# Moving a preparation phase behind the first matmuls, and splitting one sine into two, in a fused FFT-filter and state-space kernel

## Chip, cores, metric

One Trainium2 chip, one core. The metric is device time in microseconds (us) from the first to the last instruction. The runs of one kernel agree within about 0.3%. A profile shows one of these runs, so its span differs a little from the median.

TensorE is written PE in the profile lines, its weight loads PEld, VectorE DVE, ScalarE ACT, GpSimd POOL. "Granted clock" is the share of TensorE's full clock that the throttle allowed, as the records show it.

## The reference, cut to what matters

The kernel computes an output and twelve gradients of a gated sum of two branches:

```python
g = sigmoid((x * gate_w).sum(-1))
a = irfft2(rfft2(x) * (w_r + 1j * w_i))          # branch A: 2-D FFT filter, S=2048, D=1024
P = exp((dt * A)[:, :, None] * arange(L))        # branch B: state space, N=128 states
K = einsum("dn,dnl,dn->dl", C, P, dt * B).real
b = fft_convolve(K, u) + u * Dskip
out = g * a + (1 - g) * b                        # and its vjp for 12 inputs
```

In the kernel the FFTs are matmuls with cosine and sine tables. Phase A is branch A, in two passes (forward and gradient). A pass has four stages; I call the first one the projection. Phase B is branch B: 8 blocks of 128 channels. In the middle of each block lies what I call the SSM stage, in which complex powers are made from an exponential and a sine/cosine pair, 8 channels (a sub-block) at a time. AtR and AtJ are the real and imaginary parts of these powers.

## The kernel before

The three places that the change touches. First, every table comes from one helper: three VectorE operations and one sine.

```python
def trig_gen(dst, c, F, u0, us, modN, cos, tmp_pool, eng=None):
    ...
    nc.vector.tensor_scalar(out=t_i[:], in0=viota[:, 0:F], ...)            # angle, integer
    nc.vector.tensor_single_scalar(out=k_i[:], in_=t_i[:], scalar=modN - 1, op=ALU.bitwise_and)
    nc.scalar.activation(out=dst, in_=k_i[:], func=ACT.Sin, scale=-TWO_PI / modN, bias=pi_b[:])
```

Second, the head of the program. It prepares phase B first, then a barrier, then the tables of phase A, then the projection.

```python
if CFG["phaseB"]:                                  # preparation for phase B
    with ExitStack() as qctx:
        ... # 16 tables of 1025 columns (PBq_c, PBq_s) -> DRAM scratch
        def load_Tq(tl, src, i_t):                 # called 6 times: 48 x (load, transpose, copy)
            for dc in range(DC):
                eng.dma_start(out=rb[:], in_=src[dc * P:(dc + 1) * P, :])
                nc.tensor.transpose(ptq[:, :], rb[:, :], ident[:, :])
                ... # copy out on VectorE or ScalarE
        ... # products of the parameters -> DRAM scratch
    tc.strict_bb_all_engine_barrier()
if CFG["phaseA"]:
    with ExitStack() as actx:
        psum = actx.enter_context(tc.tile_pool(name="psumA", bufs=2, space=bass.MemoryType.PSUM))
        ...
        for c in range(DC):
            trig_gen(PA_c[:, c, :], ...); trig_gen(PA_s[:, c, :], ...)
        for c in range(MC):
            trig_gen(OA_c[:, c, :], ...); trig_gen(OA_s[:, c, :], ...)     # not used by the projection
```

Third, the SSM stage. A block has 4 groups (`tg`) of 4 sub-blocks (`sbl`).

```python
for tg in range(NTG):
    Tsb = bm.tile([P, DG, 4, C16], dt.bfloat16, name="Tsb")
    EAg = bm.tile([P, TG, Ds * N], dt.bfloat16, name="EAg")                # pool: one buffer
    for sbl in range(TG):
        pz0, pz1 = bcast_rows(zr2_scr, dg0, "pE", "pF")
        nc.scalar.activation(out=EAg[:, sbl, 0:HNF], in_=pz0[:, :], func=ACT.Exp, ...)
        nc.scalar.activation(out=EAg[:, sbl, HNF:2 * HNF], in_=pz1[:, :], func=ACT.Exp, ...)
    for sbl in range(TG):
        pp0, pp1 = bcast_rows(phi2_scr, dg0, "pG", "pH")
        Ts = ssmp.tile([P, Ds * N], dt.int32, name="Ts")                   # one buffer
        ... # two ScalarE copies PSUM -> Ts
        FsFc = ssmp.tile([P, 2, Ds * N], dt.int32, name="FsFc")            # one buffer
        nc.vector.tensor_single_scalar(out=FsFc[:, 0, :], in_=Ts[:], ..., op=ALU.bitwise_and)
        nc.vector.tensor_single_scalar(out=Ts[:], in_=Ts[:], ..., op=ALU.add)
        nc.vector.tensor_single_scalar(out=FsFc[:, 1, :], in_=Ts[:], ..., op=ALU.bitwise_and)
        scv = ssmp.tile([P, 2, Ds * N], dt.bfloat16, name="scv")           # one buffer
        nc.scalar.activation(out=scv[:], in_=FsFc[:], func=ACT.Sin, ...)   # both halves at once
        nc.vector.tensor_tensor(out=AtR[:], in0=EAg[:, sbl, :], in1=scv[:, 1, :], op=ALU.mult)
        nc.vector.tensor_tensor(out=AtJ[:], in0=EAg[:, sbl, :], in1=scv[:, 0, :], op=ALU.mult)
        for q in range(Ds // NQ):
            ... # 4 x (transpose of AtR, transpose of AtJ), 2 copies to Ad, 24 small matmuls
        ... # KT_blk <- psK on VectorE; Tsb <- psT on ScalarE
    # end of the group: products and reductions over the four sub-blocks
    nc.vector.tensor_tensor(out=p1[:], in0=Bcat1[:, gdl, :, :], in1=T12, op=ALU.mult)
    nc.vector.tensor_reduce(out=res4[:, 0, :], in_=p1[:]..., axis=AX.X, op=ALU.add)
    ... # three more such pairs, and T3 = T12 * erow + T34
```

Of the kernel before, what the change touches and what calls it, by code (L numbers as in the profile page):

```python
# [10 lines left out]
dt = mybir.dt  # L11
ACT = mybir.ActivationFunctionType
ALU = mybir.AluOpType
# [6 lines left out]
def kernel(  # L20
# [10 lines left out]
    nc = tc.nc  # L31
    P = 128
# [89 lines left out]
    if CFG["phaseB"]:  # L122
        with ExitStack() as qctx:
            psQ = qctx.enter_context(tc.tile_pool(name="psumQ", bufs=1, space=bass.MemoryType.PSUM))
            qpool = qctx.enter_context(tc.tile_pool(name="q_const", bufs=1))
            PBq_c = qpool.tile([P, MC, SH + 1], dt.bfloat16, name="PBq_c")
            PBq_s = qpool.tile([P, MC, SH + 1], dt.bfloat16, name="PBq_s")
            with tc.tile_pool(name="trig_tmpQ", bufs=2) as ttmp:
                for c in range(MC):
                    trig_gen(PBq_c[:, c, :], c, SH + 1, 0, 1, S, True, ttmp)  # L130
                    trig_gen(PBq_s[:, c, :], c, SH + 1, 0, 1, S, False, ttmp)
            nc.sync.dma_start(out=pb_scr[0, :, :], in_=PBq_c[:].rearrange("p a b -> p (a b)"))
            nc.scalar.dma_start(out=pb_scr[1, :, :], in_=PBq_s[:].rearrange("p a b -> p (a b)"))

            def load_Tq(tl, src, i_t):
                with tc.tile_pool(name=f"ldTq{i_t}", bufs=2) as ldp:
                    for dc in range(DC):
                        rb = ldp.tile([P, N], dt.bfloat16, name="ldT_rows")
                        eng = nc.sync if (i_t + dc) % 2 == 0 else nc.scalar
                        eng.dma_start(out=rb[:], in_=src[dc * P:(dc + 1) * P, :])  # L140
                        ptq = psQ.tile([P, P], dt.bfloat16, name=("qG" if dc % 2 == 0 else "qH"))
                        nc.tensor.transpose(ptq[:, :], rb[:, :], ident[:, :])
                        if dc % 2 == 0:
                            nc.vector.tensor_copy(out=tl[:, dc * P:(dc + 1) * P], in_=ptq[:, :])
                        else:
                            nc.scalar.activation(out=tl[:, dc * P:(dc + 1) * P], in_=ptq[:, :], func=ACT.Copy)
            ArTq = qpool.tile([P, D], dt.bfloat16, name="ArTq")
            AiTq = qpool.tile([P, D], dt.bfloat16, name="AiTq")
            load_Tq(ArTq, B_A_re, 0)
            load_Tq(AiTq, B_A_im, 1)  # L150
            nc.sync.dma_start(out=nlb_scr[0, :, :], in_=ArTq[:])
            nc.scalar.dma_start(out=nlb_scr[1, :, :], in_=AiTq[:])
            zr_q = qpool.tile([P, D], dt.float32, name="zr_q")
            phi_q = qpool.tile([P, D], dt.float32, name="phi_q")
            wR_q = qpool.tile([P, D], dt.float32, name="wR_q")
            wJ_q = qpool.tile([P, D], dt.float32, name="wJ_q")
            with tc.tile_pool(name="wtmp", bufs=1) as wtmp:
                dt_b0 = wtmp.tile([P, D], dt.float32, name="dt_b0")
                nc.gpsimd.dma_start(out=dt_b0[:], in_=B_log_dt.partition_broadcast(P))
                nc.scalar.activation(out=dt_b0[:], in_=dt_b0[:], func=ACT.Exp)  # L160
                nc.vector.tensor_tensor(out=zr_q[:], in0=dt_b0[:], in1=ArTq[:], op=ALU.mult)
                nc.vector.tensor_tensor(out=phi_q[:], in0=dt_b0[:], in1=AiTq[:], op=ALU.mult)
                nc.vector.tensor_scalar(out=phi_q[:], in0=phi_q[:], scalar1=-1.0 / TWO_PI, scalar2=None, op0=ALU.mult)
                BrT0 = wtmp.tile([P, D], dt.bfloat16, name="BrT0")
                BiT0 = wtmp.tile([P, D], dt.bfloat16, name="BiT0")
                CrT0 = wtmp.tile([P, D], dt.bfloat16, name="CrT0")
                CiT0 = wtmp.tile([P, D], dt.bfloat16, name="CiT0")
# [4 lines left out]
                dBr = wtmp.tile([P, D], dt.float32, name="dBr")  # L172
                dBi = wtmp.tile([P, D], dt.float32, name="dBi")
                nc.vector.tensor_tensor(out=dBr[:], in0=dt_b0[:], in1=BrT0[:], op=ALU.mult)
                nc.vector.tensor_tensor(out=dBi[:], in0=dt_b0[:], in1=BiT0[:], op=ALU.mult)
                t1 = wtmp.tile([P, D], dt.float32, name="t1")
                t2 = wtmp.tile([P, D], dt.float32, name="t2")
                nc.vector.tensor_tensor(out=t1[:], in0=CrT0[:], in1=dBr[:], op=ALU.mult)
                nc.vector.tensor_tensor(out=t2[:], in0=CiT0[:], in1=dBi[:], op=ALU.mult)
                nc.vector.tensor_tensor(out=wR_q[:], in0=t1[:], in1=t2[:], op=ALU.subtract)  # L180
                nc.vector.tensor_tensor(out=t1[:], in0=CrT0[:], in1=dBi[:], op=ALU.mult)
                nc.vector.tensor_tensor(out=t2[:], in0=CiT0[:], in1=dBr[:], op=ALU.mult)
                nc.vector.tensor_tensor(out=wJ_q[:], in0=t1[:], in1=t2[:], op=ALU.add)
                nc.vector.tensor_scalar(out=wJ_q[:], in0=wJ_q[:], scalar1=-1.0, scalar2=None, op0=ALU.mult)
                nc.sync.dma_start(out=nl_scr[0, :, :], in_=zr_q[:])
                nc.scalar.dma_start(out=nl_scr[1, :, :], in_=phi_q[:])
                nc.sync.dma_start(out=nl_scr[2, :, :], in_=wR_q[:])
                nc.scalar.dma_start(out=nl_scr[3, :, :], in_=wJ_q[:])
                ldt = wtmp.tile([P, DC], dt.float32, name="ldt")
                nc.gpsimd.dma_start(out=ldt[:], in_=B_log_dt.rearrange("(c p) -> p c", p=P))  # L190
                nc.scalar.activation(out=ldt[:], in_=ldt[:], func=ACT.Exp)
                nldt = wtmp.tile([P, DC], dt.float32, name="nldt")
                nc.vector.tensor_scalar(out=nldt[:], in0=ldt[:], scalar1=-1.0 / TWO_PI, scalar2=None, op0=ALU.mult)
                with tc.tile_pool(name="dl_tmp", bufs=2) as dtmp:
                    for dc in range(DC):
                        ar = dtmp.tile([P, N], dt.bfloat16, name="ar")
                        ai = dtmp.tile([P, N], dt.bfloat16, name="ai")
                        nc.sync.dma_start(out=ar[:], in_=B_A_re[dc * P:(dc + 1) * P, :])
                        nc.scalar.dma_start(out=ai[:], in_=B_A_im[dc * P:(dc + 1) * P, :])
                        for (srcb, sclt, dstscr) in ((ar, ldt, zr2_scr), (ai, nldt, phi2_scr)):  # L200
                            vf = dtmp.tile([P, N], dt.float32, name="vf")
                            nc.vector.tensor_scalar(out=vf[:], in0=srcb[:], scalar1=sclt[:, dc:dc + 1], scalar2=None, op0=ALU.mult)
                            vhi = dtmp.tile([P, N], dt.bfloat16, name="vhi")
                            nc.vector.tensor_copy(out=vhi[:], in_=vf[:])
                            vlo = dtmp.tile([P, N], dt.bfloat16, name="vlo")
                            nc.vector.tensor_tensor(out=vlo[:], in0=vf[:], in1=vhi[:], op=ALU.subtract)
                            nc.sync.dma_start(out=dstscr[0, dc * P:(dc + 1) * P, :], in_=vhi[:])
                            nc.scalar.dma_start(out=dstscr[1, dc * P:(dc + 1) * P, :], in_=vlo[:])
        tc.strict_bb_all_engine_barrier()

    if CFG["phaseA"]:
        with ExitStack() as actx:
# [6 lines left out]
            with tc.tile_pool(name="trig_tmp", bufs=2) as ttmp:  # L219
# [3 lines left out]
                for c in range(MC):  # L223
                    trig_gen(OA_c[:, c, :], c, SH, 1, 2, S, True, ttmp)
                    trig_gen(OA_s[:, c, :], c, SH, 1, 2, S, False, ttmp)
# [14 lines left out]
            def run_pass(bwd: bool):  # L240
                with ExitStack() as pctx:
                    x1pool = tc.alloc_tile_pool(name="x1pool", bufs=1, side="right")
                    X1 = x1pool.tile([P, 2, MC, NCOL], dt.bfloat16, name="X1")
                    with tc.tile_pool(name="xtpool", bufs=1, side="right") as xtpool, tc.tile_pool(name="xcpool", bufs=3, side="right") as xcpool:
# [3 lines left out]
                        for pi in range(2):  # L248
                            for mc in range(MC):
# [8 lines left out]
                                for dg in range(0, DC, TB):  # L258
                                    nb = min(TB, DC - dg)
                                    ptq = psum.tile([P, TB, P], dt.bfloat16, name="pt_tr")  # L260
# [6 lines left out]
                        for pi in range(2):  # L267
                            for mc in range(MC):
# [8 lines left out]
                                for (kind, kb) in blocks:  # L277
                                    if kind == "N":
                                        pt = psum.tile([P, 2], dt.float32, name="pt_n")
# [22 lines left out]
                                if CFG.get("dbg"):  # L302
                                    dbg = CFG["dbg"]
                                    rr = (pi * MC + mc) * P
                                    nc.sync.dma_start(out=dbg[6 if bwd else 5][rr:rr + P, :], in_=X1[:, pi, mc, :])
                    zpool = tc.alloc_tile_pool(name="zpool", bufs=1, side="left")
                    Zt = zpool.tile([P, 2, 2, QC, NCOL], dt.bfloat16, name="Zt")
                    with tc.tile_pool(name="t2y", bufs=2, side="right") as ypool, tc.tile_pool(name="t2w", bufs=2, side="right") as wpool, \
                            tc.tile_pool(name="t2e", bufs=2, side="right") as epool:
                        for rho in range(2):  # L310
                            for qc in range(QC):
# [49 lines left out]
                                pN = psum.tile([P, 8], dt.float32, name="pt_n")  # L361
# [213 lines left out]
    if CFG["phaseB"]:  # L575
# [13 lines left out]
        with ExitStack() as bctx:  # L589
# [177 lines left out]
            for bi in range(NBLK):  # L767
# [82 lines left out]
                with tc.tile_pool(name="ssm", bufs=1, side="right") as ssmp, tc.tile_pool(name="ssm2", bufs=2, side="right") as ssm2, \  # L850
# [11 lines left out]
                    for tg in range(NTG):  # L862
                        Tsb = bm.tile([P, DG, 4, C16], dt.bfloat16, name="Tsb")
                        EAg = bm.tile([P, TG, Ds * N], dt.bfloat16, name="EAg")
                        for sbl in range(TG):
                            dg0 = d0 + (tg * TG + sbl) * Ds
                            pz0, pz1 = bcast_rows(zr2_scr, dg0, "pE", "pF")
                            nc.scalar.activation(out=EAg[:, sbl, 0:HNF], in_=pz0[:, :], func=ACT.Exp, scale=twop[:, 0:1])
                            nc.scalar.activation(out=EAg[:, sbl, HNF:2 * HNF], in_=pz1[:, :], func=ACT.Exp, scale=twop[:, 0:1])
                        for sbl in range(TG):  # L870
# [5 lines left out]
                            Ts = ssmp.tile([P, Ds * N], dt.int32, name="Ts")  # L876
                            nc.scalar.activation(out=Ts[:, 0:HNF], in_=pp0[:, :], func=ACT.Copy, scale=twopK[:, 0:1])  # L877
                            nc.scalar.activation(out=Ts[:, HNF:2 * HNF], in_=pp1[:, :], func=ACT.Copy, scale=twopK[:, 0:1])
                            FsFc = ssmp.tile([P, 2, Ds * N], dt.int32, name="FsFc")
                            nc.vector.tensor_single_scalar(out=FsFc[:, 0, :], in_=Ts[:], scalar=(2 ** KFA) - 1, op=ALU.bitwise_and)  # L880
                            nc.vector.tensor_single_scalar(out=Ts[:], in_=Ts[:], scalar=(2 ** KFA) // 4, op=ALU.add)
                            nc.vector.tensor_single_scalar(out=FsFc[:, 1, :], in_=Ts[:], scalar=(2 ** KFA) - 1, op=ALU.bitwise_and)  # L882
                            scv = ssmp.tile([P, 2, Ds * N], dt.bfloat16, name="scv")
# [244 lines left out]
```

## Time and profile before

| before | value |
|---|---|
| median of 4 runs | 4043.17 us (4037.72 to 4046.75) |
| first projection matmul | 137.3 us |
| phase B starts | 1042.7 us |
| SSM stage of block 1 (the first) | 1126 to 1300 = 174 us |

These lines are from the profile page of the kernel before: its span, busy time by engine, and TensorE's busy tenths in 40 slices of 101 us each.

```profile
span 4041.1 us, 56685 instructions
PE 2512.0 (62%) x22306; PEld 1599.3 (40%) x22388; DVE 2589.3 (64%) x5625; ACT 1275.9 (32%) x1840; POOL 140.6 (3%) x277
PE   1599999894465565566556556655654755565552
```

No engine is full on average, and the averages mix three regimes. The last line shows them: a poor first slice and a half-full second one, then seven nearly full slices (phase A), then thirty-one at about half (phase B and the gap before it).

The view of busy time by windows gives two of the regimes in numbers. Columns: stretch, its length, busy time of each engine with its number of instructions, granted clock, share of the DMA engines, GB/s.

```profile
core 0: us, PE busy (x) PEld busy (x) DVE busy (x) ACT busy (x) POOL busy (x), PEclk, DMA share, GB/s
0.00:50.00 50.00, 2.79 (x14) 1.29 (x14) 24.57 (x63) 21.03 (x23) 2.96 (x10) 1.00 0.28 105
50.00:100.00 50.00, 8.83 (x36) 3.40 (x35) 19.25 (x42) 7.31 (x21) 1.60 (x2) 1.00 0.30 84
1126.00:1300.00 174.00, 96.34 (x1146) 61.91 (x1147) 118.52 (x201) 89.32 (x104) 16.16 (x32) 0.52 0.02 3
```

In the first 100 us no engine is busy for even half of the time: small loads follow one another. In the SSM stage VectorE works 118.5 of 174 us, and no other engine works more. A chain that passes from engine to engine sets that time, not a full engine.

The groups of instructions by line show the two ends of the chain waiting for each other. Columns: what, count | busy us, mean ns | idle time of the engine just before, and what ended most of it.

```profile
L884 ACT ACTIVATE scv<-FsFc,pi_b 128x2048 bf16<-128x2048 int32 x128 | 256.2, 2002 | 193.7 <-DVE FsFc L882 187.8
L884 ACT ACT_TABLE_LOAD x32 | 41.1, 1283 | 103.8 <-DVE FsFc L882 103.6
L887 DVE TENSOR_TENSOR AtR<-EAg,scv 128x1024 bf16<-128x1024 bf16 x128 | 88.6, 692 | 235.5 <-ACT scv L884 235.5
```

ScalarE sits idle 188 us in front of the sine (L884) for the masks that VectorE makes, and another 104 us for them in front of the table load that comes before the first sine of each group. VectorE sits idle 235 us for the sine. One link in order of time, from the timeline of VectorE and then of ScalarE (start, duration; in brackets the idle time before and what ended it):

```profile
1159.37 0.68 DVE L882 TENSOR_SCALAR FsFc<-Ts 128x1024 int32<-128x1024 int32 x1
1162.18 0.69 DVE L887 TENSOR_TENSOR AtR<-EAg,scv 128x1024 bf16<-128x1024 bf16 x1 [1.93 <-ACT scv L884]
...
1153.00 2.00 ACT L884 ACTIVATE scv<-FsFc,pi_b 128x2048 bf16<-128x2048 int32 x1 [1.78 <-DVE FsFc L882]
1160.15 2.00 ACT L884 ACTIVATE scv<-FsFc,pi_b 128x2048 bf16<-128x2048 int32 x1 [1.14 <-DVE FsFc L882]
```

The second mask is done at about 1160.05, the sine starts at 1160.15 and takes 2.00 us, and AtR starts at 1162.18. The next sub-block's mask may be written only when this sine has read the last one, since both tiles have one buffer. Successive AtR of one group start 6.0, 8.7 and 7.1 us apart, and 19.0 us lie between the last AtR of a group and the first of the next: 40.8 us per group.

A sine of 2048 columns at 2002 ns agrees with the Trainium skill (page "ScalarE: Activation LUTs", section "What ACT_TABLE_LOAD costs"), which puts an ACTIVATE with a bias pointer near 280 ns plus 0.833 ns per element, 1990 ns here. By the same formula two sines of 1024 cost the engine one fixed part more, which is an estimate.

### The profile page before, as it was taken

The page shows a single profiled execution, that of the slowest core. Times are in us where ns is not written, and L with a number is a line of the kernel's source. Part 1 is how long each engine was busy: PE and PEld are TensorE (multiplying, and loading weights), DVE is VectorE, ACT ScalarE, POOL GpSimd, SP SyncE. Part 2 cuts the span into 40 slices and gives each one's busy share as a digit, 9 for nine tenths or more (in the row PEclk, how much of TensorE's full clock was granted, in tenths as well). Part 3 has the DMA queues.
Part 4 walks back from the last instruction along what each step waited for, and adds up shares of the span by engine and source line. Part 5 has one row for each costly group of instructions (what it writes and reads, how often), then busy time and mean ns, then how long its engine had stood idle before and what let it go on. Part 6 is the DMA issues. An engine that isn't in the chain of part 4 may idle for free. (4 is left out here: it accounts for less than half of the span.)

```text
span 4041.1 us, 56685 instructions
## 1 busy us (share of the span) xinstructions
PE 2512.0 (62%) x22306; PEld 1599.3 (40%) x22388; DVE 2589.3 (64%) x5625; ACT 1275.9 (32%) x1840; POOL 140.6 (3%) x277
## 2 busy tenths in 40 slices
PE   1599999894465565566556556655654755565552
PEld 0344444441333443444344344434433533443431
DVE  4743218630657867885776788577668856866765
ACT  2511131010354135134414523440452345045300
POOL 0000000000010001000000000000000000001000
PEclk9999999997755775685577568657855865785565
DMA  2110012105200100010010001001000100100041
GB/s 95 54 58 27 24 61 79 47 14 112 84 3 3 32 2 4 10 23 3 3 32 1 3 6 28 3 3 32 1 3 4 31 2 3 22 12 3 3 150 49
DMA packets 199521, 114.16 MB, mean 28 GB/s; under 512 B 163795, under 2 KB 176083, under 8 KB 198614
## 3 DMA queue, kind: packets, MB, share of 16 engines
q1 hardware_dynamic: 105782, 63.26, 5.5%
q10 hardware_dynamic: 82592, 36.22, 3.4%
q0 software_dynamic: 10880, 11.06, 1.5%
q8 instruction: 175, 2.87, 0.3%
q14 instruction: 92, 0.75, 0.1%
HBM read 64.53 MB, written 45.12 MB: 27 GB/s over the span
## 5 line engine op out<-in xcount | busy, mean ns | idle before, releaser
L762 PEld LDWEIGHTS <-PB_c 128*128 128x128 bf16 x2048 | 219.1, 109 | 360.8 <-issue 246.4
L898 PE MATMUL pC<-ident,AtR 128*128 128x128 bf16 x1024 | 166.4, 304 | 244.5 <-DVE AtR L887 244.5
L884 ACT ACTIVATE scv<-FsFc,pi_b 128x2048 bf16<-128x2048 int32 x128 | 256.2, 2002 | 193.7 <-DVE FsFc L882 187.8
L898 PEld LDWEIGHTS <-AtR 128*128 128x128 bf16 x1024 | 94.6, 130 | 466.8 <-DVE AtR L887 466.8
L762 PE MATMUL pA<-HRt,PB_c 128*128 128x256 bf16 (+1 forms) x512 | 126.8, 302 | 232.7 <-issue 149.0
L887 DVE TENSOR_TENSOR AtR<-EAg,scv 128x1024 bf16<-128x1024 bf16 x128 | 88.6, 692 | 235.5 <-ACT scv L884 235.5
L763 PEld LDWEIGHTS <-PB_s 128*128 128x128 bf16 x2048 | 224.1, 110 | 27.8 <-issue 1.8
L859 PE MATMUL pG<-bc_rows,ones_row 2*128 2x512 bf16 x128 | 75.6, 591 | 246.0 <-ACT Ts L877 211.1
L667 PEld LDWEIGHTS <-PB_c 128*128 128x128 bf16 x1024 | 98.5, 114 | 259.5 <-issue 172.1
L804 ACT ACT_TABLE_LOAD x32 | 41.1, 1283 | 491.1 <-DMA out_dram<-o0c 470.3
L914 PE MATMUL pB<-GK_blk,AtR 128*128 128x16 bf16 x2048 | 185.9, 196 | 0.0
L763 PE MATMUL pA<-HJt,PB_s 128*128 128x256 bf16 (+1 forms) x512 | 126.1, 303 | 82.9 <-DVE HJt L755 72.5
L914 PEld LDWEIGHTS <-AtR 128*128 128x128 bf16 x2048 | 165.7, 115 | 0.0
L914 PE MATMUL pB<-GK_blk,AtJ 128*128 128x16 bf16 x2048 | 165.2, 193 | 0.0
L899 PE MATMUL pD<-ident,AtJ 128*128 128x128 bf16 x1024 | 163.3, 305 | 0.0
L667 PE MATMUL pA<-xg_blk,PB_c 128*128 128x256 bf16 x256 | 40.7, 313 | 195.7 <-DVE FsB L808 91.2
L914 PEld LDWEIGHTS <-AtJ 128*128 128x128 bf16 x2048 | 153.9, 113 | 0.0
L854 POOL DMA_DIRECT2D bc_rows<-zr_scr x128 | 65.4, 512 | 2477.0 <-ACT GK_blk L844 1702.7
L917 ACT ACTIVATE Tsb<-pB 128x512 bf16<-128x512 f32 x128 | 75.7, 592 | 233.3 <-PE pB L914 233.3
L859 PEld LDWEIGHTS <-ones_row 2*128 2x128 bf16 x512 | 42.9, 104 | 268.7 <-DMA bc_rows<-zr_scr 96.6
L902 DVE COPY Ad<-pD 128x512 bf16<-128x512 bf16 x256 | 108.2, 423 | 53.4 <-PE pD L899 48.6
L901 DVE COPY Ad<-pC 128x512 bf16<-128x512 bf16 x256 | 108.3, 423 | 43.8 <-PE pC L898 30.7
(529 smaller groups left out, 7373.3 us busy)
## 6 DMA issues: line engine op xcount, KB each, us to landing
Wr_t<-in_A_w_r_dram SPq DMA_DIRECT2D x32, 128.2 KB, 2.8
Wi_t<-in_A_w_i_dram ACTq DMA_DIRECT2D x32, 128.2 KB, 2.6
Yf<-y_scr SPq DMA_DIRECT2D x16, 256.5 KB, 2.7
out_dram<-wt POOLq DMA_DIRECT2D x2, 2052.0 KB, 11.9
a_scr<-och SPq DMA_DIRECT2D x16, 256.0 KB, 2.0
gx_scr<-och SPq DMA_DIRECT2D x16, 256.0 KB, 2.0
ach<-a_scr SPq DMA_DIRECT2D x128, 32.0 KB, 1.9
xga<-gx_scr ACTq DMA_DIRECT2D x128, 32.0 KB, 2.0
```

Of the source, the lines that this page charges most:

```text
L667: nc.tensor.matmul(pER[:, :], lhsT=PB_c[:, mc, ksl], rhs=v[:, 0, mc, :], start=(mc == 0), stop=(mc == MC - 1))
L762: nc.tensor.matmul(pt[:, :], lhsT=PB_c[:, c, nsl], rhs=HRt[:, c, :], start=(i == 0), stop=(i == nmm - 1)); i += 1
L763: nc.tensor.matmul(pt[:, :], lhsT=PB_s[:, c, nsl], rhs=HJt[:, c, :], start=(i == 0), stop=(i == nmm - 1)); i += 1
L859: nc.tensor.matmul(pst[:, :], lhsT=ones_row[:, :], rhs=rows[:, hh * HNF:(hh + 1) * HNF], start=True, stop=True)
L884: nc.scalar.activation(out=scv[:], in_=FsFc[:], func=ACT.Sin, scale=-TWO_PI / (2 ** KFA), bias=pi_b[:])
L887: nc.vector.tensor_tensor(out=AtR[:], in0=EAg[:, sbl, :], in1=scv[:, 1, :], op=ALU.mult)
L898: nc.tensor.transpose(ptrR[:, j, :], AtR[:, nsl], ident[:, :])
L899: nc.tensor.transpose(ptrJ[:, j, :], AtJ[:, nsl], ident[:, :])
L901: nc.vector.tensor_copy(out=Ad[:, 0, :, :], in_=ptrR[:, :, :])
L902: nc.vector.tensor_copy(out=Ad[:, 1, :, :], in_=ptrJ[:, :, :])
L914: nc.tensor.matmul(psT[:, tcols], lhsT=lt[:, nsl], rhs=rt, start=True, stop=True)
L917: nc.scalar.activation(out=Tsb[:, dsg, :, :].rearrange("p d g c -> p (d g c)"), in_=psT[:, :], func=ACT.Copy)
```

## The change

Its intent is to let TensorE start at once, and to shorten the SSM chain. The preparation becomes a function with smaller pools, called between the projection and the second stage of the first pass. The second half of the tables (OA, called the odd tables below) moves behind the projection too. The barrier goes. Two PSUM tags of phase A go to one buffer so that the preparation's PSUM fits. In the SSM stage the sine is split in two, each with its own mask and result; Ts and EAg get two buffers; a rule orders the next group's exponentials behind the last sine; and AtJ's transposes and matmuls go ahead of AtR's.

```diff
-    if CFG["phaseB"]:
+    def emit_preB():                                    # body: same work, smaller pools
...
-        tc.strict_bb_all_engine_barrier()
...
-                for c in range(MC):
-                    trig_gen(OA_c[:, c, :], c, SH, 1, 2, S, True, ttmp)
-                    trig_gen(OA_s[:, c, :], c, SH, 1, 2, S, False, ttmp)
+            def after_t1_fwd(): ...                     # the same 16 tables
...
-                                    ptq = psum.tile([P, TB, P], dt.bfloat16, name="pt_tr")
+                                    ptq = psum.tile([P, TB, P], dt.bfloat16, name="pt_tr", bufs=1)
-                                        pt = psum.tile([P, 2], dt.float32, name="pt_n")
+                                        pt = psum.tile([P, 2], dt.float32, name="pt_n", bufs=1)
...                                                      # after the projection:
+                    if not bwd:
+                        after_t1_fwd()
                     zpool = tc.alloc_tile_pool(name="zpool", bufs=1, side="left")
                     Zt = zpool.tile([P, 2, 2, QC, NCOL], dt.bfloat16, name="Zt")
+                    if not bwd:
+                        emit_preB()
...                                                      # SSM stage:
-                        EAg = bm.tile([P, TG, Ds * N], dt.bfloat16, name="EAg")
+                        EAg = bm.tile([P, TG, Ds * N], dt.bfloat16, name="EAg", bufs=2)
...
+                            if tg > 0:
+                                for ex in (exp0, exp1):
+                                    tc.add_manual_dep(ex.ins, last_sin.ins.name, ..., reason="exp after sin")
...
-                            Ts = ssmp.tile([P, Ds * N], dt.int32, name="Ts")
+                            Ts = ssmp.tile([P, Ds * N], dt.int32, name="Ts", bufs=2)
-                            FsFc = ssmp.tile([P, 2, Ds * N], dt.int32, name="FsFc")
-                            ... three VectorE operations, then
-                            nc.scalar.activation(out=scv[:], in_=FsFc[:], func=ACT.Sin, ...)
+                            nc.vector.tensor_single_scalar(out=Fs[:], in_=Ts[:], ..., op=ALU.bitwise_and)
+                            nc.scalar.activation(out=sS[:], in_=Fs[:], func=ACT.Sin, ...)
+                            nc.vector.tensor_single_scalar(out=Ts[:], in_=Ts[:], ..., op=ALU.add)
+                            nc.vector.tensor_single_scalar(out=Fc[:], in_=Ts[:], ..., op=ALU.bitwise_and)
+                            last_sin = nc.scalar.activation(out=sC[:], in_=Fc[:], func=ACT.Sin, ...)
+                            nc.vector.tensor_tensor(out=AtJ[:], in0=EAg[:, sbl, :], in1=sS[:], op=ALU.mult)
+                            nc.vector.tensor_tensor(out=AtR[:], in0=EAg[:, sbl, :], in1=sC[:], op=ALU.mult)
...                                                      # transposes: 4 of AtJ, then 4 of AtR
```

## The prediction

> **What bounds the kernel now.** Three regimes. (1) 0 to 122 us: preparation behind an all-engine barrier. The view of busy time by windows gives PE 2.8 and 8.8 of the first two 50 us; the timeline shows one 128x128 load, transpose and copy after another, about 2 us each. The first input transpose runs at 122.2 us, the first projection matmul at 137.2, the first complete groups at 143.0. (2) 143 to 951 us: phase A, PE-bound (64.6 of 72.8, 119.4 of 120.2 and 129.4 of 130.0 us busy in its first three stages, clock near 1.0). (3) Phase B, 8 blocks. In each, the SSM stage takes 174 us (1126 to 1300), with DVE 118.5, PE 96.3, ACT 89.3 busy: no engine is full, a chain is. By start times of the 2.00 us sine, a group of four sub-blocks repeats every 40.8 us: 6.0 + 8.7 + 7.2 inside, 19.0 at the group boundary. The chain: scale copy, three DVE integer ops (0.69 each), one sine of both halves, two multiplies, transposes, copies. Ts, FsFc, scv and EAg have one buffer. The waits: DVE on sine 29.3 us, sine on FsFc 24.1 plus 12.9 (its table load), final copy on PE 29.2.
>
> **What the change does.**
> - Head: preparation and the second half of the tables move behind phase A's start. The first table ops now queue behind three gate products (DVE 1.2 us each) that need gate_w and rows, landing at 4 to 5 us. So 8.5 us, then 16 table pairs at 1.5 plus 2 to 3 us of others: first groups complete near 38 us instead of 143, 105 us earlier.
> - Given back: about 55 us of DVE work, my estimate from the trace's durations (16 tables at 1.5, the parameter products and splits), now runs in the first pass's second stage, whose own DVE work is 62.9 of 120 us. It fits, but 48 transposes and in-order DMA waits on ACT and DVE sit in front of PSUM evacuations: I charge 20 us. Single pt_tr and pt_n banks: 2 us in the first pass, 4 in the second. Net phase A gain: about 80 us.
> - SSM stage: two sines of 1024 (1.15 us by the table sines of 1025), each after its own mask; Ts and EAg doubled; AtJ's transposes start before AtR exists. Instruction counts hardly change. Inside a group I chain AtR, transposes, copies, next cosine mask, copy, AtJ, KT, AtR: about 5.6 us per sub-block (21.9 becomes 16.8 for three). At the boundary the exponentials still follow the last sine; the Trainium skill (ScalarE: Activation LUTs, "Table sets: the hidden batching unit") says to batch by set, and the program keeps its 118 loads (1283 ns each in the trace). There DVE's reductions, in order, hold the multiplies: 19.0 becomes about 16.5. Per block 4 x 5.0 + 3 x 2.4 = 27 us, times 8 = 216 us.
> - Other stages of phase B, the roughly 80 us gap near 951 to 1033 us and the tail are untouched.
>
> **Prediction.** 4043 - 80 - 216 = about 3750; I say 3760, range 3680 to 3870. Chance of over 2% faster 0.96, within 2% 0.03, slower 0.01.
>
> **What would show it.** First projection group complete near 38 us; pass one's second stage near 113 to 253 us; SSM stage 140 to 155 us with group period 32 to 35; sine waits on masks nearly gone; DVE above 75% there; loads still 118.
>
> **What would make it wrong.** In-order ACT DMA issues stalling PE in the second stage by more than 40 us; PE's half clock there (0.52) making transposes and copies the chain, so that a sub-block stays at 6.5 us or more; row broadcasts (two row buffers, 1.7 us DMA) setting the boundary; or better overlap, toward DVE's 118 us, gaining more than 35 us per block.

## The result, and the profile after

| | before | after |
|---|---|---|
| median, same rounds | 4043.42 us (13 runs) | 3691.75 us (8 runs) |
| ratio | | 0.913, 95% interval 0.9121 to 0.9139 |
| first projection matmul | 137.3 | 13.8 |
| second stage starts, first pass | 215.8 | 94.3 |
| third stage starts, first pass | 339.4 | 230.5 |
| fourth stage starts, first pass | 463.9 | 355.0 |
| phase B starts | 1042.7 | 931.5 |
| block period of phase B, AtR to AtR | 357.6 | 327.7 |

A ratio is the mean time of one kernel's runs over that of the other's runs in the same rounds, so it is not quite the ratio of the medians quoted. The starts are read from the timeline, as the first matmul of each stage; the block period is the mean of the seven periods of a run. The result was correct.

The same lines of the page as before:

```profile
span 3690.1 us, 56735 instructions
PE 2493.1 (68%) x22304; PEld 1589.2 (43%) x22388; DVE 2563.5 (69%) x5624; ACT 1308.2 (35%) x1968; POOL 146.1 (4%) x277
PE   7999998991665666566656656765666566666553
```

Each engine's busy time is nearly what it was (ScalarE has 32 us more), so the 351 us came out of waiting. The busy time by windows:

```profile
core 0: us, PE busy (x) PEld busy (x) DVE busy (x) ACT busy (x) POOL busy (x), PEclk, DMA share, GB/s
0.00:50.00 50.00, 29.59 (x184) 15.08 (x188) 43.55 (x128) 31.61 (x38) 2.06 (x10) 0.93 0.19 63
50.00:100.00 50.00, 49.57 (x349) 25.27 (x354) 44.51 (x119) 41.94 (x56) 0.00 (x0) 1.00 0.23 78
1016.00:1161.00 145.00, 96.61 (x1154) 62.56 (x1155) 117.30 (x202) 93.56 (x119) 17.39 (x32) 0.53 0.02 4
```

The SSM stage of block 1 is 145 us instead of 174 with the same busy time and the same clock. VectorE is now at 81% there. In the groups of instructions, the sine's line has become two:

```profile
L890 ACT ACTIVATE sC<-Fc,pi_b 128x1024 bf16<-128x1024 int32 x128 | 146.9, 1147 | 84.3 <-DVE Fc L889 82.1
L887 ACT ACTIVATE sS<-Fs,pi_b 128x1024 bf16<-128x1024 int32 x128 | 146.8, 1147 | 61.7 <-DVE Fs L886 60.5
```

Together they are busy 294 us against 256, 37 us more. Their idle time for masks is 143 us; before it was 188 us, plus the 104 us in front of the table loads; no table load waits for a mask now. The other side of the chain changed more. VectorE, which had idled 235 us for the sine in front of AtR, now idles 15 us in front of AtJ and 8 in front of AtR over the whole run:

```profile
L892 DVE TENSOR_TENSOR AtR<-EAg,sC 128x1024 bf16<-128x1024 bf16 x128 | 87.9, 687 | 8.2 <-ACT sC L890 8.2
L891 DVE TENSOR_TENSOR AtJ<-EAg,sS 128x1024 bf16<-128x1024 bf16 x128 | 87.3, 682 | 15.3 <-ACT sS L887 15.3
```

One sub-block on VectorE and ScalarE:

```profile
1070.12 0.69 DVE L892 TENSOR_TENSOR AtR<-EAg,sC 128x1024 bf16<-128x1024 bf16 x1
1071.05 0.69 DVE L888 TENSOR_SCALAR Ts<-Ts 128x1024 int32<-128x1024 int32 x1
1072.70 0.68 DVE L889 TENSOR_SCALAR Fc<-Ts 128x1024 int32<-128x1024 int32 x1
1074.66 0.69 DVE L892 TENSOR_TENSOR AtR<-EAg,sC 128x1024 bf16<-128x1024 bf16 x1
...
1070.52 1.14 ACT L887 ACTIVATE sS<-Fs,pi_b 128x1024 bf16<-128x1024 int32 x1
1073.48 1.15 ACT L890 ACTIVATE sC<-Fc,pi_b 128x1024 bf16<-128x1024 int32 x1
```

The sine sS runs (1070.52 to 1071.66) while VectorE still works on the other half. AtR then follows without a wait, 4.5 us after the one before it. In block 1's middle groups the spacings are 6.8, 4.5 and 5.6 us, with 16.1 us at the boundary: 33.0 us per group instead of 40.8.

The account, by these marks: the start of the second stage comes 121.5 us earlier; the second stage takes 136.3 instead of 123.6 us (12.7 back); phase B starts 111.2 us earlier; and 8 blocks of 29.9 us give 239. That is 350 of 352 us.

### The profile page after: what moved, and what is told of

Same layout as the page of the kernel before. It is cut to its first block, busy times and chain, and to the rows that moved or that the text cites. A ratio compares the mean times of both kernels' runs of the same rounds, so it can differ in the third digit from the quotient of the medians.

```text
span 3690.1 us, 56735 instructions
## 1 busy us (share of the span) xinstructions
PE 2493.1 (68%) x22304; PEld 1589.2 (43%) x22388; DVE 2563.5 (69%) x5624; ACT 1308.2 (35%) x1968; POOL 146.1 (4%) x277
## 4 chain that ended last, share of the span: by engine, by line
PE 43%; DVE 34%; DMA 9%; issue 9%; ACT 4%; SPq 0%; ACTq 0%; DVEq 0%; POOL 0%; POOLq 0%
PE pC L904 3%; PE pB L919 3%; PE pA L761 2%; DVE AtR L892 2%; PE pA L760 2%; PE pD L901 2%; PE pE L536 2%; PE pB L761 2%; PE pB L760 2%; PE pE L538 1%; PE pE L289 1%; DMA go_blk<-in_grad_out_dram 1%; DVE AtJ L891 1%; PE pO L289 1%; PE pC L761 1%
## 5 line engine op out<-in xcount | busy, mean ns | idle before, releaser
L802 ACT ACT_TABLE_LOAD x32 | 41.1, 1283 | 491.3 <-DMA out_dram<-o0c 470.4
L901 PE MATMUL pD<-ident,AtJ 128*128 128x128 bf16 x1024 | 153.4, 305 | 78.3 <-DVE AtJ L891 78.3
L904 PE MATMUL pC<-ident,AtR 128*128 128x128 bf16 x1024 | 152.8, 304 | 35.7 <-DVE AtR L892 34.6
L890 ACT ACTIVATE sC<-Fc,pi_b 128x1024 bf16<-128x1024 int32 x128 | 146.9, 1147 | 84.3 <-DVE Fc L889 82.1
L887 ACT ACTIVATE sS<-Fs,pi_b 128x1024 bf16<-128x1024 int32 x128 | 146.8, 1147 | 61.7 <-DVE Fs L886 60.5
L919 PEld LDWEIGHTS <-AtJ 128*128 128x128 bf16 x2048 | 160.1, 118 | 0.0
L901 PEld LDWEIGHTS <-AtJ 128*128 128x128 bf16 x1024 | 89.1, 129 | 155.4 <-DVE AtJ L891 93.8
L919 PE MATMUL pB<-GK_blk,AtR 128*128 128x16 bf16 x2048 | 154.7, 194 | 0.0
L919 PEld LDWEIGHTS <-AtR 128*128 128x128 bf16 x2048 | 141.3, 112 | 0.0
L886 DVE TENSOR_SCALAR Fs<-Ts 128x1024 int32<-128x1024 int32 x128 | 87.8, 686 | 74.5 <-ACT Ts L879 74.5
```

The source lines that it names most:

```text
L886: nc.vector.tensor_single_scalar(out=Fs[:], in_=Ts[:], scalar=(2 ** KFA) - 1, op=ALU.bitwise_and)
L887: nc.scalar.activation(out=sS[:], in_=Fs[:], func=ACT.Sin, scale=-TWO_PI / (2 ** KFA), bias=pi_b[:])
L890: last_sin = nc.scalar.activation(out=sC[:], in_=Fc[:], func=ACT.Sin, scale=-TWO_PI / (2 ** KFA), bias=pi_b[:])
L901: nc.tensor.transpose(ptrJ[:, j, :], AtJ[:, dl * N:(dl + 1) * N], ident[:, :])
L904: nc.tensor.transpose(ptrR[:, j, :], AtR[:, dl * N:(dl + 1) * N], ident[:, :])
L919: nc.tensor.matmul(psT[:, tcols], lhsT=lt[:, nsl], rhs=rt, start=True, stop=True)
```

## The experiments

All ran with the kernel before on the same chip in the same rounds (medians 4042.10 to 4043.45 us there). All were correct except where said. "Changed kernel" is the kernel after, 3691.75 us; it was not run again in these rounds, which ran on four chips, but the medians of the kernel before agree there within 1.4 us. A spacing or a boundary is always from start to start of AtR, in block 1 of the profiled run.

### 1 and 2: each half of the change alone

Edit of the first: the changed head and phase A with the old SSM loop. Edit of the second: the old head with the changed SSM loop.

> The change before phase B alone (preparation moved, odd tables after the projection), with the SSM loop of before. Theory: the two halves add. The traces put 111 us of the gain before the first forward transform of phase B (1042.6 to 931.5 us), so 3925 to 3940 us, with the SSM group period back at 40.8 us. Rival: the halves share their gain (the preparation's DMAs or bank changes help or hurt phase B): more than 15 us off 3932.

> The new SSM loop alone on the old head. Theory: 8 blocks times 29.9 us = 239 us, so 3797 to 3811 us, group period 33.0 us. Rival: part of the SSM gain needs the new head: above 3820 us.

Measured: 3924.44 us (ratio 0.971, 0.9695 to 0.9724) and 3800.26 us (0.9404, 0.939 to 0.9418). Against 4042.14 that is 118 and 242 us, together 360; the whole change gives 350. The first lies 0.6 us outside the theory's range, the second inside it, and the group periods are 40.8 and 33.1 us as expected. The halves are nearly independent (they share 9 us), and both exceed what the prediction had for them (80 and 216).

### 3: odd tables before the projection again

```diff
                     trig_gen(PA_c[:, c, :], ...); trig_gen(PA_s[:, c, :], ...)
+                for c in range(MC):
+                    trig_gen(OA_c[:, c, :], ...); trig_gen(OA_s[:, c, :], ...)
...
-                    if not bwd:
-                        after_t1_fwd()
```

I had seen that the stretch from the first complete projection groups to the second stage fell from 72.8 us (143.0 to 215.8) to 55.3 (39 to 94.3), and thought that the odd tables had left it.

> After, with the odd tables emitted before the projection again (the preparation stays moved). Theory: the part of the head gain that the prediction missed (the projection took 81.8 us from the first table sine to the second stage, 93.9 before) comes from getting the odd tables out of the projection's way on DVE and ACT: about 12 us slower than after, 3704, second stage starting near 106 us instead of 94. Rival: it comes from the rest (gate products first, denser PE): within 4 us of after, 3692.

Measured: 3694.42 us (0.914, 0.9126 to 0.9153). The rival won. The lines below, from TensorE's timeline, show why the question was wrong: the first projection matmul and the first matmul of the second stage, of the kernel before,

```profile
137.32 0.63 PE L295 MATMUL pE<-PA_c,xT 128*128 128x512 bf16 x1
215.81 0.38 PE L324 MATMUL pE<-X,PA_c 128*128 128x512 bf16 x1
```

of the changed kernel,

```profile
13.82 0.63 PE L289 MATMUL pE<-PA_c,xT 128*128 128x512 bf16 x1
94.27 0.38 PE L322 MATMUL pE<-X,PA_c 128*128 128x512 bf16 x1
```

and the second of them in this run:

```profile
97.54 0.38 PE L317 MATMUL pE<-X,PA_c 128*128 128x512 bf16 x1
```

From its first matmul the projection takes 78.5 us before and 80.5 after. It did not shrink. What moved was my mark: "first complete groups" comes 6 us after the first matmul in one kernel and some 25 us after it in the other. In between, TensorE is busy 5.5 us in the first kernel and 17.9 us in the second (view by windows). The odd tables cost 3.3 us on the second stage's start (97.5 against 94.3); the 2.7 us in the total are within the noise. Moving the preparation and dropping the barrier were not taken apart.

### 4: the preparation one stage later

```diff
-                    if not bwd:
-                        emit_preB()              # before the second stage
...
+                    if not bwd:
+                        emit_preB()              # before the third stage
```

> After, with the preparation emitted before the first pass's third stage instead of before its second. Theory: its bill of 13 us in the second stage (133.3 against 120.2 us) is the crowding of DVE there (95.6 of 133 us busy, against 41.6 of 127.5 in the third stage), so the second stage returns to 120 to 122 us, the third grows by 0 to 5 us, and the total is 3680 to 3687. Rival: the bill is the transposes and in-order DMA waits, which stall PE in whichever stage holds them: third stage 138 us or more, total within 3 us of 3692.

Measured: 3680.7 us (0.911, 0.9094 to 0.9125), 11 us faster than the changed kernel, as the theory said. Busy time by windows of the second and third stages, first of the changed kernel, then of this run:

```profile
94.30:227.50 133.20, 124.42 (x991) 61.95 (x1004) 95.51 (x284) 34.36 (x63) 1.59 (x2) 1.00 0.47 130
227.50:355.00 127.50, 126.92 (x637) 57.53 (x646) 41.61 (x72) 18.22 (x27) 0.00 (x0) 1.00 0.01 5
```

```profile
94.70:215.00 120.30, 119.44 (x944) 60.33 (x957) 81.83 (x248) 27.55 (x38) 1.59 (x2) 1.00 0.39 109
215.00:346.00 131.00, 129.97 (x684) 60.29 (x695) 56.60 (x107) 24.80 (x51) 0.00 (x0) 1.00 0.12 36
```

These windows end some 3 us before the third stage's first matmul. From first matmul to first matmul, the second stage takes 123.7 us in this run (123.6 before the change, 136.3 in the changed kernel) and the third 127.9 us (124.5 in both others). In the kernel before, the third stage had 42.9 us of VectorE work and the second 62.9, so there is more room in the third; it grows by 3.4 us only. TensorE is over 99% busy in both stages of this run. So the preparation's bill depends on where it lies, and most of it can be avoided.

### 5: one sine again

```diff
-   Fs, Fc = two int32 tiles;  sS, sC = two bf16 tiles;  two sines of 1024
+   FsFc = ssmp.tile([P, 2, Ds * N], dt.int32, name="FsFc")
+   scv = ssmp.tile([P, 2, Ds * N], dt.bfloat16, name="scv")
+   last_sin = nc.scalar.activation(out=scv[:], in_=FsFc[:], func=ACT.Sin, ...)
```

All else is as in the changed kernel: two buffers of Ts and EAg, the rule, AtJ first.

> After, with one sine over both halves (2048) again; doubled Ts and EAg and the new order of the transposes stay. Theory: splitting the sine, with a buffer for each mask, is what shortens the sub-block, for with one mask buffer the masks of the next sub-block wait for the whole sine of this one: most of the 239 us is lost, 3830 to 3930 us, period 38 us or more. Rival: the doubled buffers give the gain: below 3740 us.

Measured: 3910.83 us (0.9675, 0.9661 to 0.9689), 219 us slower than the changed kernel, so 219 of the 242 us of the SSM half hang on the split. The mutual wait is back:

```profile
1117.29 2.00 ACT L887 ACTIVATE scv<-FsFc,pi_b 128x2048 bf16<-128x2048 int32 x1 [1.81 <-DVE FsFc L886]
...
1111.04 0.69 DVE L888 TENSOR_TENSOR AtJ<-EAg,scv 128x1024 bf16<-128x1024 bf16 x1 [2.56 <-ACT scv L887]
```

The spacings are 8.3, 7.1, 7.1 us, with 17.8 at the boundary: the old chain. The two buffers of Ts and EAg and the new order alone leave 14 us of gain over the first run (3924 us). The run merges three things at once (sine, mask tile, result tile) and does not separate them.

### 6: one buffer of Ts

```diff
-   Ts = ssmp.tile([P, Ds * N], dt.int32, name="Ts", bufs=2)
+   Ts = ssmp.tile([P, Ds * N], dt.int32, name="Ts")
```

> After, with one Ts buffer. Theory (split sine): Ts of the next sub-block waits for the cosine mask of this one, which is early enough for its sine mask in most places: 3692 to 3740 us. Rival (double buffers): the sine mask of the next sub-block comes late by a scale copy pair (1.25 us) in every sub-block, 128 times: 3800 us or more.

Measured: 3717.02 us (0.9193, 0.918 to 0.9207). The second buffer of Ts is worth 25 us on top of the split. That lies inside the theory's range. The spacings were 5.7, 7.1 and 6.5 us (sum 19.3 against 16.9), and the boundary 15.0. From the first to the last AtR a block takes 7.7 us more (121.5 against 113.8, means), and from there to the next block 4.3 less. VectorE and ScalarE run their instructions in another order here too, so the buffer and the order are not taken apart.

### 7: one buffer of EAg

```diff
-   EAg = bm.tile([P, TG, Ds * N], dt.bfloat16, name="EAg", bufs=2)
+   EAg = bm.tile([P, TG, Ds * N], dt.bfloat16, name="EAg")
```

> After, with one EAg buffer. Theory: worth nothing, because the exponentials of the next group are held behind the last sine anyway, and start (1081.6 us) 0.6 us after the last multiply that reads EAg has ended (1081.0): within 5 us of 3692. Rival: the second buffer gives the gain at the group boundary: 8 x 3 x 2.5 = 60 us slower.

Measured: 3670.52 us (0.9079, 0.9065 to 0.9092). A miss: one buffer is 21 us *faster*. The block period is 325.2 instead of 327.7 us. The boundary is 16.6 instead of 16.1, but the spacing after it is 5.1 instead of 6.8. The first four lines below are the changed kernel just after a boundary, the last two this run, just after one of its own.

```profile
1098.60 0.68 DVE L888 TENSOR_SCALAR Ts<-Ts 128x1024 int32<-128x1024 int32 x1
1100.22 0.42 DVE L906 COPY Ad<-pD 128x512 bf16<-128x512 bf16 x1 [0.94 <-PE pD L901]
1101.20 0.68 DVE L889 TENSOR_SCALAR Fc<-Ts 128x1024 int32<-128x1024 int32 x1
1101.98 1.15 ACT L890 ACTIVATE sC<-Fc,pi_b 128x1024 bf16<-128x1024 int32 x1 [2.24 <-DVE Fc L889]
```

```profile
1063.61 0.69 DVE L889 TENSOR_SCALAR Fc<-Ts 128x1024 int32<-128x1024 int32 x1
1064.39 1.15 ACT L890 ACTIVATE sC<-Fc,pi_b 128x1024 bf16<-128x1024 int32 x1
```

In the changed kernel the mask Fc stands in VectorE's queue behind a copy that waits 0.94 us for transposes, and the second cosine of the group waits 2.24 us for it. In this run Fc comes straight after the work before it, and the cosine does not wait. The second buffer frees nothing: the rule keeps the next exponentials behind the last cosine anyway, and the last AtR of the group (which frees the single buffer) starts when that cosine ends and takes 0.7 us. What differs is the order of instructions that the program's scheduler chose on ScalarE and VectorE after the first boundary. That the order, and not the buffer, makes the gain is read from the two timelines; no run changed the order alone. It covers 1.4 of the 2.5 us per block, those between a block's first and last AtR; where the other 1.1 come from is open. With one buffer the rule is idle too: built without it (not run), the program has the same instructions in the same order on every engine.

### 8: the old order of transposes

```diff
-   4 transposes of AtJ, then 4 of AtR; copies J, R; matmuls J, J, R, R
+   transposes R, J, R, J, ...;          copies R, J; matmuls R, J, R, J
```

> After, with transposes and small matmuls of AtR and AtJ interleaved as before. Theory: all of PE's part of a sub-block waits for AtR again, so four transposes (0.4 to 0.6 us) move behind AtR in each of 128 sub-blocks: 3740 to 3770 us. Rival: hidden behind DVE, which is 81% busy: within 10 us of 3692.

Measured: 3691.46 us (0.9133, 0.9118 to 0.9148), equal to the changed kernel. The rival won. The spacings of the middle groups (6.8, 4.6, 5.7, boundary 16.2) are those of the changed kernel within 0.1 us. Putting AtJ's matmuls first bought nothing.

### 9: without the ordering rule

```diff
-   if tg > 0:
-       for ex in (exp0, exp1):
-           tc.add_manual_dep(ex.ins, last_sin.ins.name, ..., reason="exp after sin")
```

> The changed kernel with two buffers of exponentials but without the added ordering rule that holds the next group's exponentials back until the last cosine-sine of this group. Built, it has 214 table loads instead of 118: the exponentials now fall between the sines. Theory (the rule is what makes the second buffer harmless: without it ScalarE pays 96 more loads of 1.28 us = 123 us, and ScalarE is on the path of each sub-block): slower than the changed kernel's 3692 us by 80 to 200 us, so 3770 to 3890. Rival (the boundary of the groups is held by the late exponentials, and taking them early is worth more than the loads cost): 3600 to 3690.

Measured: 3721.29 us (0.9203, 0.919 to 0.9217). The sign was that of the theory, the size a miss: 30 us, not 80 to 200. In the stage ScalarE is busy 108.8 of 145 us instead of 93.6, and the boundary falls to 14.7 us as the rival had it, but the spacings inside a group are 9.1, 4.0 and 6.4 us, 19.5 in sum against 16.9. Three boundaries in each of 8 blocks, 1.4 us shorter each, give back some 34 us, so the net loss of 30 us means about 64 us lost elsewhere. By this estimate about half of the added 123 us of table loads fell into time in which ScalarE was idle.

### 10: exponentials of two groups at once

```diff
-   EAg = bm.tile([P, TG, Ds * N], ..., bufs=2)                  # every group
+   if tg % 2 == 0:
+       EAg8 = bm.tile([P, 2 * TG, Ds * N], ...)                 # every second group
+   EAg = EAg8[:, (tg % 2) * TG:(tg % 2 + 1) * TG, :]
+   for sbl in range(2 * TG if tg % 2 == 0 else 0): ...          # 16 exponentials, then none
```

> The changed kernel with the exponentials of two groups (8 sub-blocks) made at once, into one tile of the same total size as the two buffers; 86 table loads instead of 118. Every second boundary between groups inside a block has no exponentials and no load at all, so ScalarE has some 7 us less to do there, and the other boundary has 8 exponentials more. It is compared with the run that has a single buffer of four exponentials (3671 us), since the instructions come in another order there too. Theory (at the boundary ScalarE's exponentials and VectorE's reductions are both near critical, and VectorE alone needs about 14 of the 16 us): 16 boundaries lose at most 2 us each and 8 gain some, so 3640 to 3680. Rival (ScalarE's exponentials alone hold the boundary): 16 boundaries lose 5 to 7 us each and the 8 long ones gain 3, so 3570 to 3620.

Measured: 3757.2 us (0.929, 0.9277 to 0.9304). Both were wrong: with 32 loads fewer it is 87 us slower than the run with one EAg buffer. The boundaries without exponentials did fall, to 13.0 and 11.2 us; the one with twice as many rose to 21.3 (16.6 in the run with one buffer). The largest loss is at the head of the stage in each block: from the first exponential to the first AtR it takes 18.9 us instead of 12.5 (means of the 8 blocks), which makes some 50 of the 87 us. The spacings beside the short boundaries grew too, to 7.5 and 8.6 us. In the line below, of ScalarE, the first cosine after a short boundary waits 7.2 us for its mask, and the two of VectorE show what the mask stood behind.

```profile
1064.51 1.15 ACT L892 ACTIVATE sC<-Fc,pi_b 128x1024 bf16<-128x1024 int32 x1 [7.20 <-DVE Fc L891]
...
1062.60 1.22 DVE L934 TENSOR_REDUCE res<-p 128x32 f32<-128x1024 bf16 x1
1063.73 0.68 DVE L891 TENSOR_SCALAR Fc<-Ts 128x1024 int32<-128x1024 int32 x1
```

The mask's input Ts was ready at 1057.3 us; the mask waited its turn in VectorE's queue, behind the products and reductions of the group before. This is what the Trainium skill says of these queues ("PSUM — Partial Sum Buffer", section "Engine vs sequencer instructions": ScalarE's and VectorE's queues are strictly first in, first out), and the trace agrees. So a boundary without exponentials takes 11 to 13 us, in the one shown because of VectorE, and the exponentials add some 3 to 5 us to that.

### 11: half of the end-of-group reductions

```diff
-   p1 = Bcat2 * T12;  res4[:, 1, :] = reduce(p1)
+   res4[:, 1, :] = copy of res4[:, 0, :]
-   p1 = Bcat2 * T3;   res4[:, 3, :] = reduce(p1)
+   res4[:, 3, :] = copy of res4[:, 2, :]
```

The result is wrong (seven of the thirteen outputs).

> The changed kernel with two of the four products and reductions at the end of each group replaced by a tiny copy; its result is wrong on purpose. VectorE has about 2 x (0.60 + 1.13) = 3.5 us less per group, 32 groups, 111 us in all. Theory (VectorE's run of reductions fills the boundary of 16.1 us, ScalarE comes close behind it): 1.5 to 3.5 us per group come off, so 3580 to 3645. Rival (ScalarE's exponentials and table loads hold the boundary): less than 0.6 us per group, 3672 to 3692.

Measured: 3635.9 us (0.8991, 0.8976 to 0.9006), 56 us faster: 1.75 us per group, inside the theory's range. But the place is not the one that the theory named. The boundary fell only from 16.1 to 15.2 us. Per block (327.7 to 320.8 us, 6.8 less; means) the stretch from the first to the last AtR lost only 1.5 us (113.8 to 112.3); the other 5.3 lie between the last AtR of a block and the first of the next, where the last group's reductions fall. At an inner boundary, taking 3.5 us of work from VectorE gave 0.9 us. The two lines below are the first AtJ after a boundary, of the changed kernel and of this run:

```profile
1095.80 0.68 DVE L891 TENSOR_TENSOR AtJ<-EAg,sS 128x1024 bf16<-128x1024 bf16 x1
1094.69 0.69 DVE L891 TENSOR_TENSOR AtJ<-EAg,sS 128x1024 bf16<-128x1024 bf16 x1 [1.53 <-ACT sS L887]
```

In the changed kernel VectorE has no idle time there; in this run it waits 1.53 us for ScalarE's sine, which comes after the exponentials and the table loads. So the two engines are nearly even at the boundary. Why the end of the block gains 5.3 us from 3.5 us of work is open.

A reduction of 128 by 1024 took 1.21 us and a product of two bf16 tiles of that size 0.68 (the reduction in run 10's lines, the products AtR and AtJ above); the product with the float32 row erow took 1.22. This agrees with the Trainium skill ("VectorE: DVE Perf Modes", section "The perf-mode tier table"): a reduction has only the slowest mode, a bf16 product runs at twice that (here 1.8 times, whole instructions compared).

### 12: the two edits that helped, together

One buffer of EAg (run 7) and the preparation before the third stage (run 4).

> The changed kernel with the two edits that each made it faster: one buffer for the exponentials of a group (3671 us alone) and the preparation for phase B emitted before the third stage of the first pass (3681 us alone). They lie in different stages, so if both gains are real and independent they add: 3692 - 21 - 11 = 3660, range 3652 to 3668. If one of them only shifted when the stages run against each other, it stays between 3668 and 3685.

Measured: 3660.84 us (0.9049, 0.9034 to 0.9064). The gains add. This version gives the correct result and is 31 us faster than the changed kernel.

## Why the prediction was right or wrong

The time predicted was 3760 us with a range of 3680 to 3870; it was 3692. The direction and the main mechanism held, and so did the range, 12 us above its lower edge. The sum was 350 us where I had 296 (80 + 216), and the terms fared differently.

- **Head, 105 us earlier: right in cause, mis-sized, 121.5 measured.** The forecast that it used, "first complete groups near 38", was met (39). The step that failed is the one from there on: that the rest of the projection takes what it took before. By that mark TensorE had already run other groups (17.9 us of work against 5.5), and it waited less afterwards, so the rest took 55.3 us instead of 72.8. The second stage, forecast near 113 to 253 us, ran from 94.3 to 230.5. From the first projection matmul (137.3 to 13.8) I would have read 123.5, less 2 us that the projection lost. Run 3 ruled out the other explanation that I tried.
- **Second stage, charge of 20 us: right in cause, 12.7 measured.** Run 4 shows that the charge comes from the preparation lying in that stage: it goes away with it, and the third stage pays 3.4 us. Which of the named parts (transposes, DMA waits, VectorE's load) makes it was not taken apart.
- **Single PSUM buffers, 2 and 4 us: not seen.** From the third stage of the first pass on, no stage lost more than 0.2 us on the change; phase B's lead over the kernel before (111.2 us) is even 2.3 us more than at the third stage (108.9). The first projection lost 2.0 us (78.5 to 80.5), but it now starts while the first table is being made (first table sine at 12.4 us, first matmul at 13.8; before at 121.9 and 137.3). No run undid these buffers alone.
- **SSM stage, 216 us: 239 measured.** Inside a group I had three spacings of 21.9 becoming 16.8 us; they became 16.9. The boundary, 19.0 to 16.5, became 16.1. The rest is in the first and last group of a block, which gained 5.7 and 6.2 us where I had 5.0. The stage took 145 us (predicted 140 to 155), the group 33.0 (32 to 35), loads stayed at 118, VectorE rose to 81% (above 75%).
- **"Sine waits on masks nearly gone": wrong.** They halved, from 291 us with the loads' waits to 143. The gain came because the wait on the other side went (235 us to 23): the split lets one half's sine run while VectorE works on the other half. Run 5 ties 219 us to it.
- **"Ts and EAg doubled" as one cause: half wrong.** The second Ts is worth 25 us (run 6). The second EAg costs 21 (run 7).
- **"AtJ's transposes start before AtR exists": no gain.** They do start earlier, but nothing waited for it (run 8).
- **DVE's reductions hold the boundary: half right.** ScalarE's exponentials hold it nearly as much (runs 10 and 11).

## What to carry to other kernels

When two engines each wait on the other, split the operation between them in two and give each half its own input and output tile: here that paid 219 us although the two sines together are 37 us longer than the one. When you move work behind a start, take the gain from the first instruction of the bounded engine, not from its first finished result, and look for a place for the moved work in a stage whose own load on the engine that it needs is light: here the stage with 42.9 us of VectorE work paid 3.4 us for it, the one with 62.9 paid 12.7. Test each extra buffer and each reordering by itself: in one loop the program was 25 us faster with one extra buffer, 21 us slower with another, and a reordering did nothing.

## What the Trainium skill lacked or had wrong

- Page "ScalarE: Activation LUTs", section "Table sets: the hidden batching unit": the rule to batch by set has no limit. Run 10 batched twice as far (86 loads instead of 118) and was 87 us slower than its partner with batches of four; some 50 us of it are the exponentials that stand before the first sine of each block (18.9 us instead of 12.5 from the first exponential to the first AtR). Run 9 added 96 loads, 123 us of ScalarE time, and lost 30 us. The loads' sum is not their price.
- Same page, sections "What ACT_TABLE_LOAD costs" and "Terms": a switch is put at about 2.7 us, load and drain. The load of 1283 ns agrees with the traces; the drain does not show: in the changed kernel a cosine ended at 1080.26, the load started at 1080.28, and the first exponential at 1081.58, 1.3 us for the switch. In 98 of the 117 loads of that run that lie between two instructions, the whole gap was under 1.5 us.
- No page says that a second buffer can lengthen a program with the order in which a scheduler then lays out the instructions: 21 us in run 7, where the order is read as the cause and not shown by a run.
- Page "VectorE: DVE Perf Modes": the tier table gives no duration for a reduction. Here 128 by 1024 bf16 took 1.21 us.
